# Decode attention and MLP in one launch: wq's load split 1 + 7 with x behind its first row, zero matmuls ahead of two stages, scores by quarters of K, one load counted on the rounds' semaphore

## The chip, the cores and the metric

The kernel runs on one core of one Trainium2 chip. A core has a matrix engine (TensorE, in the profile PE, its weight loads PEld), a vector engine (DVE), a scalar engine (ACT), GpSimd (POOL) and a synchronising engine (SP). All loads go through DMA queues that run on 16 DMA engines; a queue is fed by the engine that issues the transfer (in the profile SPq or ACTq). The metric is device time in microseconds (us) of one execution, as the median of several runs. A profiled execution gives a span, from the first to the last instruction, and that execution's own device time, which is a little longer than its span.

## The reference

One token is decoded, in bf16. `x` has 1024 elements and is layer-normed to `xn`. The result is `x + A(xn) + B(xn)`.

```
A:  q = xn @ wq                      # wq [1024, 4096], 32 heads of 128
    k, v = last 4096 rows of the caches, 4 kv heads, each shared by 8 heads
    p = softmax(q k^T / sqrt(128))
    return (p v) @ wo                # wo [4096, 1024]
B:  y = layernorm(xn)
    h = gelu(y @ w1 + b1)            # w1 [1024, 3584]
    return h @ w2 + b2               # w2 [3584, 1024]
```

Every weight is used once, so the work is 39.86 MB read from HBM for matrix products with one row: wq 8.39 MB, K 4.19, w1 7.34, V 4.19, w2 7.34, wo 8.39.

## The kernel before

All loops run over weights that are loaded once, in big transfers that SP issues in an order written out by hand (`load_chunks`, `load_k`, lines 155 to 161 and 230 to 237, and lines 308 to 319). One transfer takes several rows of the weight for each of the 128 partitions. The order is wq rows 0 to 3, K half 0, wq rows 4 to 7, K half 1, w1, both halves of V, w2 in two parts (16 and 12 chunks of 256 KB), wo in four parts (16, 11, 4 and 1 chunks of 256 KB). The three small rows x, b2 and b1 go out on ACT's queue at the very start (lines 165 to 170). A load signals a semaphore of its own by 16 when it has landed. Some issues wait: V overwrites K in SBUF, so both its halves wait for the last transposition of K (line 309); w2 overwrites wq, so it waits until q is done (line 312); wo waits until the product with w1 is done (line 314). SP takes its instructions in order, so a wait there holds back every later issue.

A product with one row is made with the weights as the moving operand, 512 columns at a time, and a nearly empty 128x128 stationary operand (XZ, YZ, GO) in which the one column in use is moved by the slice, so that each matmul adds its result into one row of a PSUM bank. `add` (line 429) records these matmuls, so most of PE's rows in the profile have line 430; they are told apart by tile: BIG,XZ is q (64 matmuls), KT,QBD the scores (32), BIG,YZ the product with w1, called h (56), KV,KT the product with V (32), BIG,GO the rounds and the tail.

PE's order is: x spread over partitions (line 426, waits for x's landing), q (lines 433 to 441), b1 and b2 and the mask put into PSUM (lines 443 to 457), scores (lines 460 to 469), h (lines 474 to 478), then the product with V, then eleven rounds (lines 497 to 503) of 8 matmuls each, seven over w2 and four over wo's first part, and then wo's last 16 chunks by matmuls of 32 columns, four at a time in the array (lines 512 to 528). PE waits on one counter, s_feed, in four places: for each half of wq, for each half of K, for each round. POOL adds to it: it waits for a load's own semaphore and then raises s_feed (lines 407 to 420).

DVE makes the layer norm of x (lines 257 to 275; XZ is done at the mark "xz"), transposes K in four quarters (`turn_k`, lines 282 to 287 and 306; three ahead of q's use and the last after it), copies q into the block diagonal QBD together with ACT (lines 298 to 305), and takes the maximum of the scores in two halves (line 330 to 333), from which the exponential follows on ACT and the transposition of p on DVE. POOL builds constants, to line 220, and QBD, XZ, GO are zeroed on it.

Of the kernel before, what the change touches and what calls it, by code (L numbers as in the profile page):

```python
# [9 lines left out]
D = 1024  # L10
# [7 lines left out]
FC = F // 128  # L18
KC = D // 128
NQ = HQ * DH  # L20
W1_CHUNKS = [8]
WQ_CHUNKS = [4, 4]
W2_CHUNKS = [16, 12]
WO_CHUNKS = [16, 11, 4, 1]
WO_HEAD = 1
XW = 136
PAIRS = 2
# [5 lines left out]
LEAD = 32  # L33
COPY = 64
ROUND = 4
ROUNDS = 11
STEP = 128

# [13 lines left out]
def bass_parallel_sum__sliding_block_cached__mixer_channel_mlp__decode_kernel(  # L52
# [17 lines left out]
    pe, dve, act, pool, sp = nc.tensor, nc.vector, nc.scalar, nc.gpsimd, nc.sync  # L70

    def sems(name, n):
        return [nc.alloc_semaphore(f"{name}{i}") for i in range(n)]

    s_x, s_b1, s_b2, s_v, s_out = (nc.alloc_semaphore(n) for n in ("s_x", "s_b1", "s_b2", "s_v", "s_out"))
    s_w1 = sems("s_w1", len(W1_CHUNKS))
    s_wq = sems("s_wq", len(WQ_CHUNKS))
    s_k = sems("s_k", PAIRS)
    s_wo = sems("s_wo", len(WO_CHUNKS))
    s_w2 = sems("s_w2", len(W2_CHUNKS))  # L80

    DVE = Track(nc, "S_DVE")
    ACT = Track(nc, "S_ACT")
    POOL = Track(nc, "S_POOL")
    done = {n: nc.alloc_semaphore(f"S_PE_{n}") for n in (
        "x", "h", "hT", "q", "sc", "pv", "tot", "fin")}
    s_feed = nc.alloc_semaphore("S_FEED")
# [5 lines left out]
    identb = sb("identb", [128, 128], bf16)  # L93
# [7 lines left out]
    OTHER = sb("OTHER", [2, 128], bf16)  # L101
    ALT = sb("ALT", [2, 512], bf16)
    EDGE = sb("EDGE", [2, 132], bf16)
    XBRP = sb("XBRP", [2, 16 * XP], bf16)
    B1R = sb("B1R", [32, F // 32], bf16)
# [6 lines left out]
    XZ = sb("XZ", [128, KC * XW], bf16)  # L112
    YZ = sb("YZ", [128, 192], bf16)
    QBD = sb("QBD", [128, PAIRS * 512], bf16)
# [15 lines left out]
    O2 = sb("O2", [128, 32], f32)  # L130
    GO = sb("GO", [128, ROUNDS * STEP + LEAD + 96], bf16)
    OT = GO[:, ROUNDS * STEP + LEAD:]
# [4 lines left out]
    BIG = sb("BIG", [128, KC * NQ + KC * F], bf16)  # L137
    WA, W1 = BIG[:, 0:KC * NQ], BIG[:, KC * NQ:KC * NQ + KC * F]
    W2 = WA[:, 0:FC * D]
    PS = nc.alloc_psum_tensor("PS", [128, 8 * 512], f32)  # L140
    PSb = PS[:, :].bitcast(bf16)

    def bank(n, rows=128, first=0):
        return PS[first:first + rows, n * 512:(n + 1) * 512]

    w1_p = B_w1.rearrange("(p r) n -> p r n", r=KC)
    wq_p = A_wq.rearrange("(p r) n -> p r n", r=KC)
    w2_p = B_w2.rearrange("(p c) n -> p c n", c=FC)
    wo_flat = A_wo.rearrange("(p j) n -> p (j n)", j=32)
# [3 lines left out]
    C = {}  # L153

    def load_chunks(dst, src, chunks, width, semaphores, c0=0):
        for j, n in enumerate(chunks):
            sp.dma_start(  # L157
                dst[:, c0 * width:(c0 + n) * width].rearrange("p (c n) -> p c n", c=n),
                src[:, c0:c0 + n, :],
            ).then_inc(semaphores[j], 16)  # L160
            c0 += n

    XB = XBRP[:, :].rearrange("p (a n) -> p a n", a=16)[:, :, 0:D // 16]

    def row_load(dst, src, semaphore):
        act.dma_start(dst, src.rearrange("o (a n) -> o a n", a=16)).then_inc(semaphore, 16)

    row_load(XB[0:1], A_x.rearrange("b s n -> (b s) n"), s_x)
    row_load(XB[1:2], B_b2.rearrange("(o n) -> o n", o=1), s_b2)
    act.dma_start(B1R[:, :], B_b1.rearrange("(p c) -> p c", p=32)).then_inc(s_b1, 16)  # L170

    def pool_wait():
        pool.wait_ge(POOL.sem, POOL.cnt)
# [45 lines left out]
    POOL.mark(pool.tensor_tensor(out=HALF[:, :], in0=HALF4[:, 0:2], in1=HALF4[:, 2:4], op=ALU.add))  # L219
    C["consts"] = POOL.cnt  # L220

    act.wait_ge(POOL.sem, C["QBD"])
    ACT.mark(act.activation(out=PS[:, 0:1024], in_=QBD[:, :], func=ACTF.Copy))
    ACT.mark(act.activation(out=bank(7), in_=QBD[:, 0:512], func=ACTF.Copy))
# [2 lines left out]
    def pairs(cache, c):  # L227
        return cache[0, 2 * c:2 * c + 2, SK - W:SK, :].rearrange("g (m i) d -> m g (i d)", m=64)

    def load_k(c):  # L230
        sp.dma_start(KV[:, c * 8192:(c + 1) * 8192], pairs(A_k_cache, c)).then_inc(s_k[c], 16)  # L231

    load_chunks(WA, wq_p, WQ_CHUNKS[:1], NQ, s_wq)
    load_k(0)
    load_chunks(WA, wq_p, WQ_CHUNKS[1:], NQ, s_wq[1:], WQ_CHUNKS[0])
    load_k(1)
    load_chunks(W1, w1_p, W1_CHUNKS, F, s_w1)

# [43 lines left out]
    def turn_k(n):  # L282
        dve.wait_ge(s_k[n // 2], 16)
        C["kt", n] = DVE.mark(dve.transpose(KT[:, n * 4096:(n + 1) * 4096], KV[:, n * 4096:(n + 1) * 4096]))  # L284

    for n in range(3):
        turn_k(n)

    act.wait_ge(done["q"], 8)
# [8 lines left out]
    for b in range(4):  # L298
        for c in range(PAIRS):
            to = QD[32 * b:32 * b + 32, c, :, b, 16 * c:16 * c + 16].rearrange("p e (u j) -> p e u j", j=4)  # L300
# [2 lines left out]
                C["d_QBD"] = DVE.mark(dve.tensor_copy(to, of))  # L303
            else:
                C["a_QBD"] = ACT.mark(act.activation(out=to, in_=of, func=ACTF.Copy))  # L305
    turn_k(3)

    V = KV[:, :]
    sp.wait_ge(DVE.sem, C["kt", 3])
    for c in range(PAIRS):  # L310
        sp.dma_start(V[:, c * 8192:(c + 1) * 8192], pairs(A_v_cache, c)).then_inc(s_v, 16)
    sp.wait_ge(done["q"], 8)
    load_chunks(W2, w2_p, W2_CHUNKS, D, s_w2)
    sp.wait_ge(done["h"], 7)
    c0 = 0
    for j, n in enumerate(WO_CHUNKS):
        first = (FC + c0) * D
        sp.dma_start(BIG[:, first:first + n * D], wo_flat[:, c0 * D:(c0 + n) * D]).then_inc(s_wo[j], 16)  # L318
        c0 += n

    def spread(first, n):
# [6 lines left out]

    S = PS[:, 3 * 512:7 * 512]
    for n in range(2):  # L330
        dve.wait_ge(done["sc"], 14 + 2 * n)
        C["mx"] = DVE.mark(dve.tensor_reduce(  # L332
            out=MX2[:, n:n + 1], in_=S[:, 1024 * n:1024 * n + 1024], axis=AX.X, op=ALU.max))
    dve_wait()
# [62 lines left out]
    for engine, track, a in ((act, ACT, 1), (dve, DVE, 0)):  # L397
        engine.wait_ge(done["fin"], 1)
        of, to = PS[64 * a:64 * a + 64, 7 * 512 + 256 * a:7 * 512 + 256 * a + 256], Pb[0:64, 256 * a:256 * a + 256]
# [4 lines left out]


    pool_wait()
    pool.wait_ge(s_wq[0], 16)
    pool.sem_inc(s_feed, 1)
    pool.wait_ge(s_wq[1], 16)
    pool.sem_inc(s_feed, 1)  # L410
    pool.wait_ge(DVE.sem, C["kt", 1])
    pool.sem_inc(s_feed, 1)
    pool.wait_ge(DVE.sem, C["kt", 3])
    pool.sem_inc(s_feed, 1)
    for semaphores, chunks in ((s_w2, W2_CHUNKS), (s_wo, WO_CHUNKS[:WO_HEAD])):
        if semaphores is s_wo:
            pool.wait_ge(ACT.sem, C["OT"])
        for semaphore, n in zip(semaphores, chunks):
            pool.wait_ge(semaphore, 16)
            pool.sem_inc(s_feed, n // ROUND)  # L420
    pe.wait_ge(POOL.sem, C["ones"])
    turn = pe.alloc_register("turn")
    pe.reg_mov(turn, 1)
    pe.wait_ge(s_x, 16)
    for i in range(2):
        last = pe.matmul(bank(2 + i), lhsT=onesb[0:1, :], rhs=XB[0:1, 8 * i:8 * i + 8, :])  # L426
    last.then_inc(done["x"], 1)

    def add(to, lhsT, rhs, **place):
        return pe.matmul(to, lhsT=lhsT, rhs=rhs, start=False, stop=False, skip_group_check=True, **place)  # L430

    pe.wait_ge(DVE.sem, C["xz"])
    with pe.Fori(0, len(WQ_CHUNKS)) as j:
        pe.wait_ge(s_feed, turn)
        pe.reg_add(turn, turn, 1)
        with pe.Fori(0, 4) as t:
            for u in range(2):
                for k in range(4):
                    last = add(bank(7), XZ[:, bass.ds(t * 2 + j * (4 * XW) + (XW * k + u), 128)],
                               WA[:, bass.ds(t * -1024 + j * (4 * NQ) + (k * NQ + (7 - u) * 512), 512)])  # L440
            last.then_inc(done["q"], 1)

    pe.wait_ge(s_b1, 16)
    turned = PS[:, 2 * 512 + 32:2 * 512 + 64].rearrange("p (c t) -> p c t", c=4)[:, :, 0:7]
    for q in range(4):
        pe.matmul(turned, lhsT=E4[:, q * 128:(q + 1) * 128],
                  rhs=B1R[:, q * FC:(q + 1) * FC].rearrange("p (t c) -> p c t", c=4),
                  start=(q == 0), stop=False, skip_group_check=True)
# [4 lines left out]
    for a in range(2):  # L453
        pe.matmul(bank(7), lhsT=EDGE[:, 1 - a:129 - a], rhs=XB[:, 8 * a:8 * a + 8, :], start=(a == 0), stop=False,
                  skip_group_check=True)
    for n in range(4):
        pe.matmul(bank(3 + n), lhsT=OTHER[:, :], rhs=ALT[:, :], start=True, stop=False, skip_group_check=True)
    pe.wait_ge(DVE.sem, C["d_QBD"])
    K4 = KT[:, :].rearrange("p (x k) -> p x k", k=128)
    with pe.Fori(0, PAIRS) as c:  # L460
        pe.wait_ge(s_feed, turn)
        pe.reg_add(turn, turn, 1)
        pe.wait_ge(ACT.sem, C["a_QBD"])
        with pe.Fori(0, 2) as j:
            for n in range(4):
                for u in range(2):
                    last = add(bank(3 + n), QBD[:, bass.ds(c * 512 + j * 256 + u * 128, 128)],
                               K4[:, bass.ds(c * 64 + 16 * n, 16), bass.ds(j * 64 + 32 * u, 32)])
                last.then_inc(done["sc"], 1)

    def h_cols(row, t):
        return row.rearrange("p (m a c) -> p m a c", m=128, a=7)[:, :, bass.ds(t, 1), :]
# [2 lines left out]
    with pe.Fori(0, 7) as t:  # L475
        for k in range(KC):
            last = add(bank(0), YZ[:, bass.ds(t + 8 * k, 128)], h_cols(W1[:, k * F:(k + 1) * F], t))
# [5 lines left out]
    for c in range(4):  # L483
        last = add(turned[:, c], H8[:, c:512:4], FLIP[:, 0:7])
# [6 lines left out]
    with pe.Fori(0, 8) as i:  # L491
        for u in range(4):
            last = add(bank(1), PT[:, bass.ds(i * 256 + u * 64, 128)], V3[:, :, bass.ds(i * 1024 + u * 256, 256)])
# [2 lines left out]
    pe.wait_ge(DVE.sem, C["d_GT"])  # L496
    with pe.Fori(0, ROUNDS) as t:
        pe.wait_ge(s_feed, turn)
        pe.reg_add(turn, turn, 1)
        for u in range(ROUND):  # L500
            for a in range(2):
                add(bank(7), GO[:, bass.ds(t * STEP + (LEAD + 2 * u - ROW - a), 128)],
                    BIG[:, bass.ds(t * (ROUND * D) + (u * D + a * 512), 512)])

    c0 = TAIL
# [54 lines left out]
```

## Time and profile before

| | |
|---|---|
| median of 3 runs | 99.41 us (99.19 to 99.42) |
| profiled execution | 99.37 us, span 97.4 us |
| PE busy | 73.0 us of the span (354 matmuls) |
| DVE busy | 38.9 us |
| ACT, POOL busy | 11.2 us, 9.9 us |
| bytes | 39.86 MB read, 409 GB/s over the span |
| SP's DMA queue | its packets' time is 95.7% of 16 engines' span |

The page gives, for each engine, the busy time in the span, then the span in 40 equal slices (each 2.4 us) with the busy share in tenths, the granted clock of PE in tenths, the busy share of the DMA engines and the GB/s they moved. Then it follows the chain of work that ended last back from the last instruction. Groups of instructions are listed by line and tile with their mean duration and what ended the idle time before them. DMA issues are listed with the time from the start of the issue to the landing. Matmuls overlap, so the duration of one (380 ns) is longer than the distance between two (about 216 ns at the full clock).

### The profile page before, as it was taken

What the parts mean: (1) busy time and instruction counts of PE and PEld (TensorE: products, weight loads), DVE (VectorE), ACT (ScalarE), POOL (GpSimd) and SP (SyncE); (2) the same over time, 40 slices, a digit from 0 to 9 for tenths busy, and PEclk for the clock granted to TensorE, in tenths of its full rate; (3) what the DMA queues carried; (4) which work ended last, traced back from release to release, by engine and by line L of the source; (5) the groups of instructions that cost most, each with busy time, mean ns of one, the idle gap of its engine ahead of it and who ended that gap; (6) DMA issues with size and microseconds to landing.
All of it is one profiled execution on the core that took longest, in us unless ns stands there. A gap on an engine that the chain in (4) does not pass through costs nothing.

```text
span 97.4 us, 1285 instructions
## 1 busy us (share of the span) xinstructions
PE 73.0 (75%) x354; PEld 30.4 (31%) x354; DVE 38.9 (40%) x54; ACT 11.2 (12%) x20; POOL 9.9 (10%) x27
## 2 busy tenths in 40 slices
PE   0004000099999986999979999799999999779992
PEld 0000000033444431333434444333343443334450
DVE  0002899899930799940293620050048000000001
ACT  0880000600000024000005200200000000000001
POOL 6999400000000000000000000000000000000000
PEclk9999999999999998557999999999999999999999
DMA  7599999999999998888999999999999999899890
GB/s 215 256 431 431 405 432 444 431 444 431 410 431 481 636 424 377 377 377 377 437 431 431 437 498 431 431 444 394 394 464 498 431 431 431 376 435 426 372 377 1
DMA packets 1989, 39.88 MB, mean 409 GB/s; under 512 B 322, under 2 KB 324, under 8 KB 452
## 3 DMA queue, kind: packets, MB, share of 16 engines
q1 hardware_dynamic: 1876, 39.85, 95.7%
q10 hardware_dynamic: 112, 0.01, 0.1%
q8 instruction: 1, 0.02, 0.1%
HBM read 39.86 MB, written 0.00 MB: 409 GB/s over the span
## 4 chain that ended last, share of the span: by engine, by line
DMA 80%; PE 14%; SPq 3%; issue 1%; DVE 0%
DMA BIG<-in_B_w_dram 47%; DMA BIG<-in_A_wo_dram 33%; PE PS L430 13%; SPq L231 1%; SPq L157 1%; SPq L318 1%; DVE Pb L400 0%; PE PS L507 0%
## 5 line engine op out<-in xcount | busy, mean ns | idle before, releaser
L430 PE MATMUL PS<-BIG,XZ 128*128 x64 | 16.5, 427 | 10.2 <-DVE B L277 10.2
L430 PE MATMUL PS<-BIG,GO 128*128 (+1 forms) x148 | 22.2, 337 | 1.4 <-POOLq L420 1.2
L284 DVE STREAM_TRANSPOSE KT<-KV 128x4096 bf16<-128x4096 bf16 x4 | 17.6, 4432 | 4.8 <-DMA KV<-in_A_k_cache_dram 4.8
L430 PEld LDWEIGHTS PS<-BIG,GO 128*128 (+1 forms) x148 | 9.9, 97 | 13.8 <-issue 6.4
L430 PEld LDWEIGHTS PS<-BIG,XZ 128*128 x64 | 6.9, 108 | 20.3 <-issue 14.3
L430 PE MATMUL PS<-BIG,YZ 128*128 x56 | 12.4, 380 | 0.6 <-DMA BIG<-in_B_w_dram 0.6
L430 PE MATMUL PS<-KT,QBD 128*128 x32 | 10.0, 491 | 1.0 <-ACT QBD L305 1.0
L430 PE MATMUL PS<-KV,KT 128*128 x32 | 8.3, 381 | 0.5
L400 DVE CAST Pb<-PS 64x256 bf16<-64x256 f32 x1 | 0.4, 417 | 20.4 <-PE PS L507 20.4
L430 PEld LDWEIGHTS PS<-BIG,YZ 128*128 x56 | 5.4, 96 | 7.6 <-issue 1.8
L426 PE MATMUL PS<-XBRP,onesb 1*128 1x512 bf16 x2 | 1.0, 616 | 8.1 <-DMA XBRP<-in_A_x_dram 8.1
L430 PEld LDWEIGHTS PS<-KT,QBD 128*128 x32 | 3.8, 120 | 7.2 <-issue 5.2
L244 DVE BATCH_NORM_STATS2 BN<-PS 128x6 f32<-128x512 f32 x2 | 1.3, 689 | 9.1 <-PE PS L426 9.1
L430 PEld LDWEIGHTS PS<-KV,KT 128*128 x32 | 3.1, 96 | 5.3 <-issue 3.8
L332 DVE TENSOR_REDUCE MX<-PS 128x1 f32<-128x1024 f32 x2 | 2.4, 1220 | 5.6 <-PE PS L430 5.6
L379 DVE SCALAR_TENSOR_TENSOR QBD<-PS,REC,HALF 32x256 f32<-32x256 f32 x2 | 0.9, 474 | 6.9 <-PE PS L430 6.8
L344 ACT ACTIVATE Pb<-PS,NMB 128x2048 bf16<-128x2048 f32 x1 | 2.0, 1968 | 13.8 <-DVE NMB L341 13.8
L348 DVE STREAM_TRANSPOSE KT<-Pb 128x2048 bf16<-128x2048 bf16 x1 | 2.3, 2311 | 2.1 <-ACT Pb L344 2.1
L353 DVE COPY HT<-PS 128x28 f32<-128x28 f32 x1 | 0.2, 210 | 6.4 <-PE PS L430 6.4
L400 ACT ACTIVATE Pb<-PS 64x256 bf16<-64x256 f32 x1 | 0.4, 381 | 20.1 <-PE PS L507 20.1
L426 PEld LDWEIGHTS PS<-XBRP,onesb 1*128 1x128 bf16 x2 | 0.1, 104 | 8.1 <-DMA XBRP<-in_A_x_dram 8.1
L290 ACT ACTIVATE Pb<-PS 128x512 bf16<-128x512 f32 x1 | 0.6, 597 | 16.6 <-PE PS L430 16.6
(77 smaller groups left out, 37.7 us busy)
## 6 DMA issues: line engine op xcount, KB each, us to landing
BIG<-in_A_wq_dram SPq DMA_DIRECT2D x2, 4096.0 KB, 18.8
BIG<-in_B_w_dram SPq DMA_DIRECT2D x1, 7168.0 KB, 46.0
KV<-in_A_k_cache_dram SPq DMA_DIRECT2D x2, 2048.0 KB, 23.1
KV<-in_A_v_cache_dram SPq DMA_DIRECT2D x2, 2048.0 KB, 13.6
BIG<-in_B_w_dram SPq DMA_DIRECT2D x1, 4096.0 KB, 24.8
BIG<-in_A_wo_dram SPq DMA_DIRECT2D x1, 4096.0 KB, 23.5
BIG<-in_B_w_dram SPq DMA_DIRECT2D x1, 3072.0 KB, 31.4
BIG<-in_A_wo_dram SPq DMA_DIRECT2D x1, 2816.0 KB, 29.8
```

The source lines that it names most:

```text
L157: sp.dma_start(dst[:, c0 * width:(c0 + n) * width].rearrange("p (c n) -> p c n", c=n), src[:, c0:c0 + n, :],).then_inc(semaphores[j], 16)
L231: sp.dma_start(KV[:, c * 8192:(c + 1) * 8192], pairs(A_k_cache, c)).then_inc(s_k[c], 16)
L244: DVE.mark(dve.bn_stats(out=BN[:, 12 * n + 6 * i:12 * n + 6 * i + 6], in_=src[:, 512 * i:512 * i + 512]))
L284: C["kt", n] = DVE.mark(dve.transpose(KT[:, n * 4096:(n + 1) * 4096], KV[:, n * 4096:(n + 1) * 4096]))
L318: sp.dma_start(BIG[:, first:first + n * D], wo_flat[:, c0 * D:(c0 + n) * D]).then_inc(s_wo[j], 16)
L332: C["mx"] = DVE.mark(dve.tensor_reduce(out=MX2[:, n:n + 1], in_=S[:, 1024 * n:1024 * n + 1024], axis=AX.X, op=ALU.max))
L344: C["exp"] = ACT.mark(act.activation(out=Pb[:, :], in_=S, func=ACTF.Exp, bias=NMB[:, 0:1], scale=SCALE, accum_out=SUMP[:, 0:1]))
L348: C["d_pt"] = DVE.mark(dve.transpose(PT[:, 0:2048], Pb[:, :]))
L379: DVE.mark(dve.scalar_tensor_tensor(out=ONM.rearrange("p (i c d) -> p i c d", i=2, c=PAIRS)[:, i], in0=PS[rows, 512:1024].rearrange("p (c ...
L400: track.mark(act.activation(out=to, in_=of, func=ACTF.Copy) if a else dve.tensor_copy(to, of))
L426: last = pe.matmul(bank(2 + i), lhsT=onesb[0:1, :], rhs=XB[0:1, 8 * i:8 * i + 8, :])
L430: return pe.matmul(to, lhsT=lhsT, rhs=rhs, start=False, stop=False, skip_group_check=True, **place)
```

## The change

- wq is loaded as one row for each partition (1 MB) and then seven (7 MB), both on one semaphore, both ahead of K. The load of x moves from ACT's queue to SP's, between the two. The loads of b2 and b1 stay on ACT's queue and wait for POOL's `identb`.
- q waits for both parts of wq directly (no s_feed) and runs in eight groups of 8 matmuls, each group over all eight rows of wq for 512 columns.
- A function `busy` adds matmuls whose stationary and moving operands are zero. 38 of them (19 times 2) run ahead of q, after POOL's constants; 8 run among the four mask matmuls ahead of the scores.
- Two quarters of K are transposed ahead of q's use, two after. The scores run by quarters of K: each waits for its own transposition, and the two halves of the maximum wait for 3 and 4 quarters in place of 14 and 16 groups.
- V's first half waits for K's second quarter, its second half for the fourth.
- s_feed counts 32 for each round. wo's first load adds its 16 to it directly, POOL the other 16 when the attention's output is ready, and then the remaining three rounds.
- wo is loaded as 16, 10, 5 and 1 chunks in place of 16, 11, 4 and 1.

```diff
-WQ_CHUNKS = [4, 4]
+WQ_CHUNKS = [1, 7]
-WO_CHUNKS = [16, 11, 4, 1]
+WO_CHUNKS = [16, 10, 5, 1]
+HALF_FEED = 16
...
-    s_wq = sems("s_wq", len(WQ_CHUNKS))
+    s_wq = [nc.alloc_semaphore("s_wq")] * len(WQ_CHUNKS)
...
-    row_load(XB[0:1], A_x.rearrange("b s n -> (b s) n"), s_x)
-    row_load(XB[1:2], B_b2.rearrange("(o n) -> o n", o=1), s_b2)
-    act.dma_start(B1R[:, :], B_b1.rearrange("(p c) -> p c", p=32)).then_inc(s_b1, 16)
...
+    act.wait_ge(POOL.sem, C["identb"])
+    row_load(act, XB[1:2], B_b2.rearrange("(o n) -> o n", o=1), s_b2)
+    act.dma_start(B1R[:, :], B_b1.rearrange("(p c) -> p c", p=32)).then_inc(s_b1, 16)
...
     load_chunks(WA, wq_p, WQ_CHUNKS[:1], NQ, s_wq)
+    row_load(sp, XB[0:1], A_x.rearrange("b s n -> (b s) n"), s_x)
+    load_chunks(WA, wq_p, WQ_CHUNKS[1:], NQ, s_wq, WQ_CHUNKS[0])
     load_k(0)
-    load_chunks(WA, wq_p, WQ_CHUNKS[1:], NQ, s_wq[1:], WQ_CHUNKS[0])
     load_k(1)
...
-    for n in range(3):
+    for n in range(2):
         turn_k(n)
...
-    turn_k(3)
+    for n in range(2, 4):
+        turn_k(n)
...
-    sp.wait_ge(DVE.sem, C["kt", 3])
     for c in range(PAIRS):
+        sp.wait_ge(DVE.sem, C["kt", 2 * c + 1])
         sp.dma_start(V[:, c * 8192:(c + 1) * 8192], pairs(A_v_cache, c)).then_inc(s_v, 16)
...
-        sp.dma_start(BIG[:, first:first + n * D], wo_flat[:, c0 * D:(c0 + n) * D]).then_inc(s_wo[j], 16)
+        sp.dma_start(BIG[:, first:first + n * D], wo_flat[:, c0 * D:(c0 + n) * D]).then_inc(s_wo[j] if j else s_feed, HALF_FEED)
...
-        dve.wait_ge(done["sc"], 14 + 2 * n)
+        dve.wait_ge(done["sc"], 3 + n)
...
+    for semaphore, n in zip(s_w2, W2_CHUNKS):
+        pool.wait_ge(semaphore, 16)
+        pool.sem_inc(s_feed, 2 * HALF_FEED * (n // ROUND))
+    pool.wait_ge(ACT.sem, C["OT"])
+    pool.sem_inc(s_feed, HALF_FEED)
+    pool.wait_ge(s_feed, 2 * HALF_FEED * (FC // ROUND + 1))
+    pool.sem_inc(s_feed, 2 * HALF_FEED * (WO_CHUNKS[0] // ROUND - 1))
...
+    def busy(zeros, to, **how):
+        for i in range(2):
+            pe.matmul(to, lhsT=zeros[:, 0:128], rhs=zeros[:, 0:512], skip_group_check=True, **how)
+
+    pe.wait_ge(POOL.sem, C["consts"])
+    with pe.Fori(0, 19):
+        busy(QBD, bank(4), start=True, stop=True)
     pe.wait_ge(DVE.sem, C["xz"])
...
+    with pe.Fori(0, 8) as t:
+        pe.wait_ge(s_wq[0], 16 * len(WQ_CHUNKS))
+        for k in range(KC):
+            last = add(bank(7), XZ[:, bass.ds(t + XW * k, 128)], WA[:, bass.ds(t * -512 + (k * NQ + 7 * 512), 512)])
+        last.then_inc(done["q"], 1)
...
+    with pe.Fori(0, 4) as n:
+        pe.matmul(PS[:, bass.ds(n * 512 + 3 * 512, 512)], lhsT=OTHER[:, :], rhs=ALT[:, :], start=True, stop=False,
+                  skip_group_check=True)
+        busy(GO, bank(1), start=False, stop=False)
...
+        with pe.Fori(0, 2) as i:
+            pe.wait_ge(DVE.sem, turn)
+            pe.reg_add(turn, turn, 1)
+            for n in range(2):
+                for j in range(2):
+                    for u in range(2):
+                        last = add(PS[:, bass.ds(i * 1024 + (3 + n) * 512, 512)],
+                                   QBD[:, bass.ds(c * 512 + (j * 256 + u * 128), 128)],
+                                   K4[:, bass.ds(c * 64 + i * 32 + 16 * n, 16), j * 64 + 32 * u:j * 64 + 32 * u + 32])
+            last.then_inc(done["sc"], 1)
...
         pe.wait_ge(s_feed, turn)
-        pe.reg_add(turn, turn, 1)
+        pe.reg_add(turn, turn, 2 * HALF_FEED)
```

More of the change, by code (lines that the diff above doesn't have):

```diff
@@ L163, in bass_parallel_sum__sliding_block_cached__mixer_channel_mlp__decode_kernel, with row_load @@
     XB = XBRP[:, :].rearrange("p (a n) -> p a n", a=16)[:, :, 0:D // 16]
-    def row_load(dst, src, semaphore):
-        act.dma_start(dst, src.rearrange("o (a n) -> o a n", a=16)).then_inc(semaphore, 16)
-    row_load(XB[0:1], A_x.rearrange("b s n -> (b s) n"), s_x)
-    row_load(XB[1:2], B_b2.rearrange("(o n) -> o n", o=1), s_b2)
-    act.dma_start(B1R[:, :], B_b1.rearrange("(p c) -> p c", p=32)).then_inc(s_b1, 16)
+    def row_load(engine, dst, src, semaphore):
+        engine.dma_start(dst, src.rearrange("o (a n) -> o a n", a=16)).then_inc(semaphore, 16)
     def pool_wait():
@@ L406, in bass_parallel_sum__sliding_block_cached__mixer_channel_mlp__decode_kernel @@
     pool_wait()
[L407 to L421, printed above, removed]
+    for semaphore, n in zip(s_w2, W2_CHUNKS):
[5 more added lines that the diff above has]
+    pool.sem_inc(s_feed, 2 * HALF_FEED * (WO_CHUNKS[0] // ROUND - 1))
+    pe.wait_ge(POOL.sem, C["QBD"])
     turn = pe.alloc_register("turn")
-    pe.reg_mov(turn, 1)
+    pe.reg_mov(turn, C["kt", 0])
     pe.wait_ge(s_x, 16)
@@ L430, in add @@
         return pe.matmul(to, lhsT=lhsT, rhs=rhs, start=False, stop=False, skip_group_check=True, **place)
-    pe.wait_ge(DVE.sem, C["xz"])
-    with pe.Fori(0, len(WQ_CHUNKS)) as j:
-        pe.wait_ge(s_feed, turn)
-        pe.reg_add(turn, turn, 1)
[L436 to L441, printed above, removed]
+    def busy(zeros, to, **how):
[4 more added lines that the diff above has]
+        busy(QBD, bank(4), start=True, stop=True)
+    pe.wait_ge(DVE.sem, C["xz"])
+    with pe.Fori(0, 8) as t:
[3 more added lines that the diff above has]
+        last.then_inc(done["q"], 1)
     pe.wait_ge(s_b1, 16)
@@ L455, in bass_parallel_sum__sliding_block_cached__mixer_channel_mlp__decode_kernel @@
                   skip_group_check=True)
-    for n in range(4):
-        pe.matmul(bank(3 + n), lhsT=OTHER[:, :], rhs=ALT[:, :], start=True, stop=False, skip_group_check=True)
+    with pe.Fori(0, 4) as n:
+        pe.matmul(PS[:, bass.ds(n * 512 + 3 * 512, 512)], lhsT=OTHER[:, :], rhs=ALT[:, :], start=True, stop=False,
+                  skip_group_check=True)
+        busy(GO, bank(1), start=False, stop=False)
     pe.wait_ge(DVE.sem, C["d_QBD"])
@@ L460, in bass_parallel_sum__sliding_block_cached__mixer_channel_mlp__decode_kernel @@
     with pe.Fori(0, PAIRS) as c:
-        pe.wait_ge(s_feed, turn)
-        pe.reg_add(turn, turn, 1)
         pe.wait_ge(ACT.sem, C["a_QBD"])
[L464 to L469, printed above, removed]
+        with pe.Fori(0, 2) as i:
[8 more added lines that the diff above has]
+            last.then_inc(done["sc"], 1)
+        pe.reg_add(turn, turn, C["kt", 2] - C["kt", 1] - 1)
+    pe.reg_mov(turn, 2 * HALF_FEED)
     def h_cols(row, t):
@@ L498, in bass_parallel_sum__sliding_block_cached__mixer_channel_mlp__decode_kernel @@
         pe.wait_ge(s_feed, turn)
-        pe.reg_add(turn, turn, 1)
+        pe.reg_add(turn, turn, 2 * HALF_FEED)
         for u in range(ROUND):
```

## The prediction

> **What bounds the kernel now.** I read the page's slices first, then the chain that ended last, then each load's landing, then the engines' timeline for the slack. Page of the profile (span and slices) and its account of queues:
>
> ```profile
> span 97.4 us, 1285 instructions
> PEclk9999999999999998557999999999999999999999
> GB/s 215 256 431 431 405 432 444 431 444 431 410 431 481 636 424 377 377 377 377 437 431 431 437 498 431 431 444 394 394 464 498 431 431 431 376 435 426 372 377 1
> q1 hardware_dynamic: 1876, 39.85, 95.7%
> ```
>
> SP's queue is busy 95.7% of 97.4 us, 93.2 us; about 2 us are missing at each end and nothing between. The loads' issues (size, time from the start of the issue to the landing) and the end of the chain, in order of time:
>
> ```profile
> BIG<-in_B_w_dram SPq DMA_DIRECT2D x1, 7168.0 KB, 46.0
> BIG<-in_A_wo_dram SPq DMA_DIRECT2D x1, 4096.0 KB, 23.5
> BIG<-in_A_wo_dram SPq DMA_DIRECT2D x1, 2816.0 KB, 29.8
> BIG<-in_A_wo_dram SPq DMA_DIRECT2D x1, 1024.0 KB, 31.8
> BIG<-in_A_wo_dram SPq DMA_DIRECT2D x1, 256.0 KB, 32.0
> ```
>
> ```profile
> 62.92 31.79 DMA BIG<-in_A_wo_dram
> 94.72 0.04 issue
> 94.76 0.62 PE PS L430 x16
> 95.38 0.02 issue
> 95.40 0.30 PE PS L507 x4
> 95.70 0.02 issue
> 95.72 0.42 DVE Pb L400
> ```
>
> wo's parts were issued at 62.08, 62.45, 62.92 and about 63.4, so they landed at 85.6, 92.3, 94.7 and 95.4. The first half of wq (issue 0.81, asked for alone 12.1 us) landed at 12.9. From there to 95.4 the other 35.66 MB took 82.5 us, 432 GB/s throughout. The kernel is one unbroken stream of loads, about 2 us before it and 2.0 us of tail behind 95.4. So an edit counts if it moves the stream's start, opens a gap in it, or makes PE too late for the last landings. PE's slack in the timeline:
>
> ```profile
> 19.33 16.55 PE L430 MATMUL PS<-BIG,XZ 128*128 x64 [10.22 <-DVE B L277]
> 24.42 9.23 PEld L430 LDWEIGHTS PS<-BIG,XZ 128*128 x43 [0.28 <-issue]
> 38.14 4.45 DVE L284 STREAM_TRANSPOSE KT<-KV 128x4096 bf16<-128x4096 bf16 x1
> 49.61 12.44 PE L430 MATMUL PS<-BIG,YZ 128*128 x56 [0.57 <-DMA BIG<-in_B_w_dram]
> 85.92 9.46 PE L430 MATMUL PS<-BIG,GO 128*128 x92 [1.18 <-POOLq L420]
> 93.23 1.10 PEld L430 LDWEIGHTS PS<-BIG,GO 128*32 128x32 bf16 x44 [0.42 <-issue]
> 94.76 0.34 PEld L430 LDWEIGHTS PS<-BIG,GO 128*32 128x32 bf16 x16 [0.43 <-DMA BIG<-in_A_wo_dram]
> 95.10 0.11 PEld L517 LDWEIGHTS <-GO 128*32 128x32 bf16 x4
> ```
>
> From h at 49.61 on PE works without a real pause until it waits 1.18 us for wo's first part and 0.43 us for the third. Those two are what a later h can use up.
>
> **The change part by part.**
>
> *Start of the stream.* SP still issues wq at 0.81. x's issue (0.58 us on ACT before) now stands between wq's two; wq's second issue ends near 2.6 instead of 1.9, and w1's near 4.5 instead of 3.9. The first megabyte keeps the queue busy until about 5, so this costs 0; uncovered it would be 0.58. Bytes are equal. One row of wq is an 8 KB run for each partition, 64 KB apart; wo's third part has the same runs at the same distance, and its megabyte took 92.3 to 94.7, 2.4 us or 430 GB/s. What the trace can't show is another first transfer. In 1 to 3 us the stream moved 360 and 164 KB, 0.52 MB where 0.86 go at 432 GB/s: 0.8 us short, of which 0.2 lie ahead of the end of wq's issue at 1.2. Ends: -0.6 if smaller runs avoid the rest, +0.6 if the start were paid again behind x. I take 0, because the nearest row, 6 to 12 us with the small packets of x, b2 and b1 in it, moved 526, 524, 526, 360, 263 and 429 GB/s, a mean of 438: small packets cost the stream nothing.
>
> *x, layer norm, ACT.* x landed at 8.0, on a queue of its own. Now it follows the first megabyte: 12.9 less 3 MB at 2.43 us is 5.6. The chain from x to XZ took 10.4 us (8.08 to 18.46), so XZ is ready near 16. ACT issues b2 and b1 (0.6 + 0.7 us) only after identb, at 2.56, so its first table load moves from 2.80 to 3.9 and its square-root table is ready near 8.1 instead of 6.94, when the variance is due (5.6 + 1.05 + 1.29 + 0.5 = 8.4): 0. b1 and b2 are wanted near 37. All of it is hidden, because q now waits for something later.
>
> *q.* All of wq, 8.39 MB, lands at 12.9 + 4.19/0.432 = 22.6, against a start of q at 19.33. POOL's constants end at 11.0, so the 38 zero matmuls start there. Before, q's matmuls stood 0.427 us apart until 24.4, and 0.215 from then (9.23/43): the gate opened 5.1 us after q began. With 12 zero matmuls at 0.427 and 26 at 0.216 they take 10.7 us, to 21.7 (8 to 16 slow ones: 20.9 to 22.6), ahead of wq. q then runs at full clock: h's 56 matmuls are 12.44 us, so 64 take 14.2. From 22.9 (0.25 from landing to first matmul, as with h) it ends at 37.1, against 35.9: +1.2 us.
>
> *K, scores.* K's first half lands with wq's old second half at 27.5, so quarters one and two are done by 27.5 + 8.76 = 36.3, before q. After q, QBD's copying took 2.2 us (35.91 to 38.14); quarters three and four then run 39.3 to 48.1, where the last one ended at 42.6. Eight zero matmuls (1.7 us) and the mask run from 37.7 to about 41; QBD is ready near 40, so scores start 1 us late, but their first three quarters (24 matmuls, 5.2 to 6.7 us) end by 47.7 and the last one has to wait for 48.1 anyway: 0. If that transposition were early, they would cost 1.
>
> The last quarter: 0.4 us of register work (38.15 to 38.98 before holds two such), 8 matmuls at 0.216 to 0.28 (the latter if the sequencer can't run ahead), 0.4 to 0.6 to leave the loops and begin h. So h begins at 50.6 to 51.2, not 49.61: 1.0 to 1.6 us late. The maximum's first half now runs ahead of that, so the exponential and p's transposition end near 58, before V's product at 64: 0.
>
> *Does that reach the end?* No: 1.18 + 0.43 us of waits, plus 0.10 for 40 narrow matmuls where 44 were (1.10/44 each), plus 0.1 at the last part: 20 loads take 0.43 where 16 took 0.34, then 0.11, so 95.3 against the landing at 95.4. Slack 1.8 against 1.0 to 1.6. The fifth chunk in wo's third part costs 0 by the same sum.
>
> *Queue waits on SP.* V's first half is issued at 36.3 (before 42.6), its second at 48.1, w2 from 48.7, wo near 63.4. w1 lands at 49.3 and a half of V lasts 4.9 us, so the second half is needed by 53, w2 by 58, wo by 75: no gap, with 5 us to spare. POOL's wait took 85.62 to 85.69, so counting directly saves under 0.1, inside the slack.
>
> Sum: 99.37 for the profiled execution (97.4 plus 1.97 around it), 0.04 below the median, plus 0: 99.4.
>
> **The rivals.** A difference below 0.3%, 0.3 us, can hardly be told from none here.
>
> 1. *PE too late* (the other side). If h starts over 1.8 us late, each further tenth is on the path: the last quarter of the scores is the place. The first weight loads of the scores stood 0.28 us apart near 39; if the output bank, which now moves too, adds 0.1 to each of 8 (an estimate: one more register step) and 0.3 are lost between the zero matmuls and q, lateness is 2.1 to 2.7 and the time 99.7 to 100.3. For it: the margin is only 0.2 to 0.8. Against it: h and q keep 0.22 for each matmul in loops of 8.
>
> 2. *The clock gate.* Either the zero matmuls don't open it, and q pays 12 x 0.21 = 2.5 us again (h 3.8 late, 2.0 over, 101.4), or it falls in a gap ahead of the last quarter (0.3 to 1.9 us) and 8 to 16 matmuls of scores and h pay 0.21 each: 1.7 to 3.4, over by 1.2 to 3.2. For it: the granted clock was 0.50 from 38.2 to 45.0 although PE was never idle over 0.96 us; between 35.9 and 38.2 it ran only matmuls of 1 to 32 rows. Against: from 83.0 to 86.4 PE was busy 2.22 of 3.40 us and the clock stayed 1.00. The Trainium skill, "TensorE: Matmul & The Clock Gate" (Part 1), lets the gate fall only after an idle window of some 3.4 us; by that rule the second case never happens and this rival keeps only its first. The trace contradicts a rule of idle time alone, so I don't lower it.
>
> 3. *A better start*: the 0.6 us above falls away, wholly or by half: 98.8 to 99.1. For it: 0.52 MB in 2 us. Against: nothing says the run's length causes that.
>
> 4. *The strided row is slow.* At half the rate the first megabyte costs 2.4 us more, on the stream: 101.8. [...] wo's third part speaks against it.
>
> **How the numbers follow.** No change that reaches the end 0.60 (its own range 99.1 to 99.7); PE late 0.12; gate 0.13; start 0.13; slow row 0.02. Faster 0.13, same 0.60, slower 0.12 + 0.13 + 0.02 = 0.27. The range takes in the better start and PE late, and the milder half of the gate's: 98.8 to 101.0.
>
> **What would show it.** Right: x at 5.6, wq at 22.6, q 22.9 to 37.1 with matmuls 0.216 apart, the last transposition to 48.1, h from about 51, the wait ahead of wo's first part almost gone, wo's last landings at 94.7 and 95.4 as before. Wrong: any of those landings moved (start), a granted clock of 0.50 in q or after 46 us, or no wait left ahead of wo's third part.

## The result, and the profile after

The changed kernel takes 100.21 us (median; 99.6 to 100.68) against 99.12 us (98.75 to 99.42) for the kernel before: a ratio of 1.0106, 95% interval 1.0076 to 1.0136. It is slower, by about 1 us, where no change was forecast. The profiled execution took 100.22 us, its span is 98.8 us.

The page after, span, slices and SP's queue:

```profile
span 98.8 us, 1412 instructions
PEclk9999999999999999859999999999999999999999
GB/s 70 634 326 465 396 373 395 371 405 418 444 424 557 541 371 395 371 418 557 265 424 431 431 484 424 424 424 405 448 448 411 424 424 438 439 406 410 406 240 2
q1 hardware_dynamic: 1908, 39.85, 94.8%
```

The queue moved the same 39.85 MB, but was busy for 94.8% of 98.8 us in place of 95.7% of 97.4. The next two fences are the end of the chain in order of time, and the loads (size, time from the start of the issue to the landing):

```profile
63.73 0.33 SPq L320
64.06 0.04 issue
64.10 0.43 SPq L320
64.54 0.04 issue
64.58 31.55 DMA BIG<-in_A_wo_dram
96.13 0.04 issue
96.17 0.73 PE PS L425 x20
96.91 0.20 PE PS L511 x4
97.10 0.02 issue
97.13 0.42 DVE Pb L402
```

```profile
BIG<-in_A_wq_dram SPq DMA_DIRECT2D x1, 1024.0 KB, 4.7
BIG<-in_A_wq_dram SPq DMA_DIRECT2D x1, 7168.0 KB, 21.8
BIG<-in_A_wo_dram SPq DMA_DIRECT2D x1, 4096.0 KB, 23.1
BIG<-in_A_wo_dram SPq DMA_DIRECT2D x1, 256.0 KB, 31.7
```

The kernel still ends on wo's landings, and these are later: the third part at 64.58 + 31.55 = 96.1, where it was 94.7, the last at 96.8, where it was 95.4. That is +1.4 us, the whole of the span's 1.4. 1.1 us of it is already there at wq: the second load, issued at 1.94, landed at 1.94 + 21.8 = 23.7, where 22.6 was forecast. The rest came later, 0.17 us of it for each DMA engine in packets near 87 us, of which the last section tells.

PE, DVE and the issue of wq in the timeline after:

```profile
1.28 0.62 SPq L167 DMA_DIRECT2D XBRP<-in_A_x_dram  x1
1.94 0.57 SPq L158 DMA_DIRECT2D BIG<-in_A_wq_dram  x1
17.23 5.06 PEld L429 LDWEIGHTS PS<-QBD 128*128 128x128 bf16 x24 [0.28 <-issue]
23.86 13.98 PE L425 MATMUL PS<-BIG,XZ 128*128 x64 [1.08 <-DMA BIG<-in_A_wq_dram]
39.97 8.77 DVE L285 STREAM_TRANSPOSE KT<-KV 128x4096 bf16<-128x4096 bf16 x2
51.27 12.44 PE L425 MATMUL PS<-BIG,YZ 128*128 x56
87.05 8.55 PE L425 MATMUL PS<-BIG,GO 128*128 x68 [0.74 <-POOLq L415]
96.17 0.45 PEld L425 LDWEIGHTS PS<-BIG,GO 128*32 128x32 bf16 x20 [0.86 <-DMA BIG<-in_A_wo_dram]
```

h begins at 51.27, 1.66 us later than before, and yet PE waits 0.74 us for wo's first part and again for the third. PE isn't what is late.

The trace also records each landing by DMA engine (16 for each load) and each packet; a packet of wq's second load is one partition's run of it, 56 KB. wq's second load landed on 15 engines between 22.3 and 23.0 and on the sixteenth at 23.70. wo's last part landed on 15 between 95.4 and 96.0 and on the sixteenth at 96.76. One engine had fallen 0.7 us behind the others before 24 us, and at each later load, for 73 us, one landed 0.6 to 0.8 us behind the fifteenth; the landings do not say which, but so steady a distance points to the same one. The packet records say when: the first packets of wq's second load, from 4.55 on, directly behind x, took 0.39 us longer on the mean of the engines than the usual 2.12, on the worst 1.15 longer. Before, no load but the very first had such packets.

### The profile page after: what moved, and what is told of

It is laid out like the page before. It is cut to its first block, busy times and chain, and to the rows that moved or that the text cites. A ratio compares the mean times of both kernels' runs of the same rounds, so it can differ in the third digit from the quotient of the medians.

```text
span 98.8 us, 1412 instructions
## 1 busy us (share of the span) xinstructions
PE 81.8 (83%) x389; PEld 34.0 (34%) x400; DVE 39.1 (40%) x54; ACT 11.2 (11%) x20; POOL 10.5 (11%) x27
## 3 DMA queue, kind: packets, MB, share of 16 engines
q1 hardware_dynamic: 1908, 39.85, 94.8%
## 4 chain that ended last, share of the span: by engine, by line
DMA 54%; PE 40%; SPq 2%; issue 1%; ACT 1%; DVE 0%
PE PS L425 35%; DMA BIG<-in_A_wo_dram 32%; DMA BIG<-in_A_wq_dram 22%; PE PS L429 3%; PE PS L455 1%; SPq L320 1%; SPq L167 1%; ACT Pb L291 1%; PE PS L452 1%; DVE Pb L402 0%; SPq L158 0%; PE PS L511 0%
## 5 line engine op out<-in xcount | busy, mean ns | idle before, releaser
L425 PE MATMUL PS<-BIG,GO 128*128 (+1 forms) x137 | 21.5, 334 | 2.0 <-POOLq L415 0.7
L429 PE MATMUL PS<-QBD 128*128 128x512 bf16 x38 | 11.1, 463 | 5.0 <-POOL HALF L216 5.0
L425 PE MATMUL PS<-BIG,XZ 128*128 x64 | 14.0, 379 | 1.1 <-DMA BIG<-in_A_wq_dram 1.1
L425 PEld LDWEIGHTS PS<-BIG,XZ 128*128 x64 | 6.2, 98 | 8.8 <-issue 2.5
L429 PEld LDWEIGHTS PS<-QBD 128*128 128x128 bf16 x38 | 4.2, 113 | 12.2 <-issue 9.5
L425 PE MATMUL PS<-KT,QBD 128*128 x32 | 7.9, 402 | 0.0
L425 PEld LDWEIGHTS PS<-KT,QBD 128*128 x32 | 3.3, 104 | 4.8 <-issue 1.9
L429 PE MATMUL PS<-GO 128*128 128x512 bf16 x8 | 3.2, 493 | 0.0
## 6 DMA issues: line engine op xcount, KB each, us to landing
BIG<-in_A_wq_dram SPq DMA_DIRECT2D x1, 7168.0 KB, 21.8
```

The source lines that it names most:

```text
L429: pe.matmul(to, lhsT=zeros[:, 0:128], rhs=zeros[:, 0:512], skip_group_check=True, **how)
```

## The experiments

Each ratio is to the kernel before, timed beside the run (its medians there were 98.88 to 98.95 us). A landing is that of the slowest engine in the profiled execution.

**Theories.** S: the stream's start is paid twice, in the first packets behind x, and a load signals only when its slowest engine is done. P: PE is too late through the last quarter of the scores (the first rival of the prediction). S splits by its cause: x's place (S1), the step from runs of 8 KB for each partition to runs of 56 KB (S2), or b2's and b1's small packets (S3).

**The old start of loads under the new kernel.** [4, 4] rows, x, b2 and b1 on ACT's queue at once; all else as changed.

```diff
-WQ_CHUNKS = [1, 7]
+WQ_CHUNKS = [4, 4]
+    row_load(act, XB[0:1], A_x.rearrange("b s n -> (b s) n"), s_x)
+    row_load(act, XB[1:2], B_b2.rearrange("(o n) -> o n", o=1), s_b2)
+    act.dma_start(B1R[:, :], B_b1.rearrange("(p c) -> p c", p=32)).then_inc(s_b1, 16)
...
-    act.wait_ge(POOL.sem, C["identb"])
-    row_load(act, XB[1:2], B_b2.rearrange("(o n) -> o n", o=1), s_b2)
-    act.dma_start(B1R[:, :], B_b1.rearrange("(p c) -> p c", p=32)).then_inc(s_b1, 16)
...
-    row_load(sp, XB[0:1], A_x.rearrange("b s n -> (b s) n"), s_x)
```

> The changed kernel with the start of loads of before: wq as 4 + 4 rows, x, b2 and b1 on ACT's queue at once; all else as changed. Theory S (the stream's start is paid twice and one DMA engine stays about 0.7 us behind): the last landing goes back from 96.8 to about 95.4 and the time to that of before, ratio 0.998 to 1.003. Rival P (PE too late through the last quarter of the scores): the time stays near 1.010.

Measured: 0.9998 (0.9984 to 1.0012), last landing 95.7. P falls: q behind all of wq (landed at 22.6), the late transpositions, the zero matmuls and the new split of wo together cost nothing. The whole loss lies in the start of the loads.

**Only x back on ACT's queue.**

```diff
+    row_load(act, XB[0:1], A_x.rearrange("b s n -> (b s) n"), s_x)
...
-    row_load(sp, XB[0:1], A_x.rearrange("b s n -> (b s) n"), s_x)
```

> Only x goes back to ACT's queue at the start; wq stays 1 + 7, b2 and b1 stay behind identb. If x between the two loads of wq makes the bubble (S1): ratio near 1.000 or below, down to 0.997, because the first packets of 8 KB cost 0.3 us less than those of 32 KB. If the step from 8 KB runs to 56 KB runs makes it (S2): ratio stays 1.006 to 1.011. P: 1.010.

Measured: 1.0002 (0.9988 to 1.0015). SP's issues and the loads:

```profile
0.81 0.87 SPq L158 DMA_DIRECT2D BIG<-in_A_wq_dram  x2
BIG<-in_A_wq_dram SPq DMA_DIRECT2D x1, 7168.0 KB, 21.4
XBRP<-in_A_x_dram ACTq DMA_DIRECT2D x1, 2.0 KB, 4.7
```

Both loads of wq are issued by 1.68, the second lands by 22.7, and x lands at 5.5, as early as on SP's queue. S2 falls: 8 KB runs with 56 KB runs behind them are still there. x on SP's queue is the cause, but not yet in which way.

**Only the split back to 4 + 4.** x stays on SP between the halves.

```diff
-WQ_CHUNKS = [1, 7]
+WQ_CHUNKS = [4, 4]
```

> Only wq's split goes back to 4 + 4; x stays on SP between the two, so it lands near 13 instead of 5.6 and XZ near 24, so that q starts near 24 instead of 23.9. S1: the packets behind x are late again, only later, ratio 1.004 to 1.010. S2: the stream is as before and PE at most 0.3 us later, ratio 1.000 to 1.004. P: 1.010 to 1.015.

Measured: 1.0068 (1.0039 to 1.0097). By its ratio alone this would be S1, and that would be wrong. In its profile wq landed by 22.6, the last part of wo at 95.6, and no packet behind x was slow. What is late there is PE: x lands at 13.2, and the zero matmuls stand behind x's on PE. PE in its timeline:

```profile
24.41 13.98 PE L425 MATMUL PS<-BIG,XZ 128*128 x64
49.80 1.90 PE L425 MATMUL PS<-KT,QBD 128*128 x8 [1.46 <-DVE KT L285]
83.80 12.05 PE L425 MATMUL PS<-BIG,GO 128*128 x105
```

q begins at 24.4, h at 51.8 (2.2 us later than before), and from there on PE waits for no load. So P is real with h this late; it is not what the change suffers from, where PE still waits. The profiled execution is this kernel's shortest (99.10 of 99.10 to 100.05 us), so how late PE was in the longer ones, and whether PE alone made them longer, isn't shown.

**b2 and b1 early.**

```diff
+    row_load(act, XB[1:2], B_b2.rearrange("(o n) -> o n", o=1), s_b2)
+    act.dma_start(B1R[:, :], B_b1.rearrange("(p c) -> p c", p=32)).then_inc(s_b1, 16)
...
-    act.wait_ge(POOL.sem, C["identb"])
-    row_load(act, XB[1:2], B_b2.rearrange("(o n) -> o n", o=1), s_b2)
-    act.dma_start(B1R[:, :], B_b1.rearrange("(p c) -> p c", p=32)).then_inc(s_b1, 16)
```

> Only b2 and b1 go back to the start of ACT's queue (without the wait for identb); x and wq as changed. If the late engine comes from b2's and b1's small packets between packets of 56 KB (S3): the spread of the landings of wq's second load shrinks from 1.4 us to about 0.5 and the ratio to 1.002 to 1.005. S1 and S2: nothing changes, 1.010.

Measured: 1.0100 (1.0075 to 1.0125), one engine 0.6 us behind the others at wq and 0.8 at the end. S3 falls. The run also shows what one engine does: on the mean of the engines wo's last part landed at 95.37, as with the old start of loads (95.37 too), on the slowest at 96.39 against 95.73.

**Two ways in which x could do it.** D: x's issue delays the issue of wq's second load, which then comes too shortly before the queue gets to it. X: x's small packets break the stream. A larger first load tells them apart, and a late issue without x.

```diff
-WQ_CHUNKS = [1, 7]
+WQ_CHUNKS = [2, 6]
```

> The changed kernel with wq as 2 + 6 rows, x still between them on SP's queue. If the bubble behind x comes from wq's second load being issued too late for a queue that is nearly dry (theory D), 2 MB of cover leave its descriptors waiting 2.4 us longer: no excess in its first packets, the last landing near 95.5, ratio 0.999 to 1.003. If x's small packets themselves break the stream wherever they stand in it (theory X): the bubble moves to 7.5 us and stays, ratio 1.006 to 1.010.

```diff
+    row_load(act, XB[0:1], A_x.rearrange("b s n -> (b s) n"), s_x)
...
-    row_load(sp, XB[0:1], A_x.rearrange("b s n -> (b s) n"), s_x)
+    sp.wait_ge(POOL.sem, C["QBD"])
     load_chunks(WA, wq_p, WQ_CHUNKS[1:], NQ, s_wq, WQ_CHUNKS[0])
```

> x on ACT's queue at the start, wq as 1 + 7, and SP waits for POOL's zeroed QBD before it issues the second load, so that this goes out near 2.05, as late as in the changed kernel (1.94), without x ahead of it. Theory D: the bubble is back without x, ratio 1.005 to 1.011. Theory X: none, ratio 0.999 to 1.002.

Measured: 1.0004 (0.9987 to 1.0021) with 2 + 6 and x in between, 1.0125 (1.0110 to 1.0141) with the late issue and x elsewhere. Both go D's way. SP's issues in the latter (the first line holds both loads of wq and the wait between them) and its loads:

```profile
0.81 1.58 SPq L158 DMA_DIRECT2D BIG<-in_A_wq_dram  x2
BIG<-in_A_wq_dram SPq DMA_DIRECT2D x1, 1024.0 KB, 4.8
BIG<-in_A_wq_dram SPq DMA_DIRECT2D x1, 7168.0 KB, 21.5
XBRP<-in_A_x_dram ACTq DMA_DIRECT2D x1, 2.0 KB, 5.0
```

**The lead varied with 2 + 6.** SP waits for a later or an earlier mark of POOL before the second load of wq; x stays in between.

```diff
-WQ_CHUNKS = [1, 7]
+WQ_CHUNKS = [2, 6]
...
-    POOL.mark(pool.memset(ALT[:, :], 0.0))
+    C["hold"] = POOL.mark(pool.memset(ALT[:, :], 0.0))
...
+    sp.wait_ge(POOL.sem, C["hold"])
     load_chunks(WA, wq_p, WQ_CHUNKS[1:], NQ, s_wq, WQ_CHUNKS[0])
```

> wq as 2 + 6 rows with x between them, and SP waits for POOL's zeroed ALT (4.7 us) before it issues the second load, which ends near 5.2. The first 2 MB keep the queue until about 7. Theory D (a load has to be issued some 2.5 us before the queue gets to it): 1.8 us of lead are too few, the stream loses 0.5 to 1.2 us there, ratio 1.005 to 1.013. If only a first transfer of 1 MB, or its 8 KB runs, makes the loss: ratio 1.000, as with 2 + 6 alone.

The second takes the mark of FLIP's zeroing instead of ALT's.

> The same with the wait on an earlier mark of POOL (3.9 us), so that the second load's issue ends near 4.5 and leads by 2.5 us. Theory D: little or no loss, ratio 0.999 to 1.004, and between the runs with 2.0 and with 4.5 us of lead. If any late issue costs alike: 1.005 or more.

Measured: 1.0124 (1.0093 to 1.0155) and 1.0001 (0.9981 to 1.0021). The issue of wq's second load, first in the late, then in the middle run:

```profile
4.71 0.34 SPq L158 DMA_DIRECT2D BIG<-in_A_wq_dram  x1
```

```profile
3.93 0.34 SPq L158 DMA_DIRECT2D BIG<-in_A_wq_dram  x1
```

0.78 us decide over 1.2%. The runs side by side; lead is from the end of the issue of wq's second load to its first packet, the excess is what the first packet of each engine took over its usual time, both from the packet records, the landings are those of the slowest engine:

| kernel | lead us | excess us, mean and worst engine | wq landed | wo's last landed | ratio |
|---|---|---|---|---|---|
| changed | 2.04 | 0.39, 1.15 | 23.70 | 96.76 | 1.0106 |
| b2 and b1 early | 2.25 | 0.14, 0.77 | 23.28 | 96.39 | 1.0100 |
| late issue, x on ACT | 2.22 | 0.76, 1.19 | 23.57 | 96.27 | 1.0125 |
| 2 + 6, late | 2.24 | 0.47, 1.16 | 23.99 | 96.69 | 1.0124 |
| x on ACT | 2.88 | 0.01, 0.10 | 22.68 | 95.49 | 1.0002 |
| 2 + 6, middle | 3.00 | 0.00, 0.00 | 22.59 | 95.61 | 1.0001 |
| 2 + 6 | 4.78 | 0.00, 0.00 | 22.69 | 95.58 | 1.0004 |

In this table a lead of 2.0 to 2.25 us costs 0.8 to 1.2 us on the worst engine, one of 2.9 or more 0.1 us at most, whatever the first load's size, its runs, or x's place.

The ratios 1.0125 and 1.0124 are not the loads' alone. In the profiles of the late issue and of the late 2 + 6 PE ran to the end with no wait, or one of 0.2 us. In the late 2 + 6 PE had stood idle for 2.78 us ahead of q, and its granted clock was 0.50 from 25.22 to 28.64:

```profile
24.15 15.67 PE L426 MATMUL PS<-BIG,XZ 128*128 x64 [2.78 <-DMA BIG<-in_A_wq_dram]
75.49 21.80 PE L426 MATMUL PS<-BIG,GO 128*128 x148
```

q took 1.7 us longer than the 13.98 of the middle run, h began at 53.25, and PE's rounds set the end. Three of its six executions show a mean granted clock of 1.000 and took 99.61 to 100.25 us, still 0.7 to 1.3 us more than the kernel before. The changed kernel and the one with b2 and b1 early end on wo's landings instead.

V's second half, which waits for the last transposition, shows the same further on. Its issue in the late 2 + 6, then in the run without zero matmuls (below):

```profile
50.75 0.54 SPq L314 DMA_DIRECT2D KV<-in_A_v_cache_dram  x1
```

```profile
49.74 0.54 SPq L314 DMA_DIRECT2D KV<-in_A_v_cache_dram  x1
```

The leads there were 2.78 and 2.82 us (first packets at 54.07 and 53.09), and the worst packets were 0.50 and 1.03 us long beyond their usual 0.61; with 3.45 us, in the run with 4 + 4, there was no excess. Whether one limit, just under 2.9 us, holds for both loads no run tests.

What happens in the engines in those 2 to 3 us no run shows. The Trainium skill, "DMA: Bandwidth & Descriptors" (Latency and other measured facts), gives about 0.6 us to the first byte of a load issued from SP and up to 2 us for an access to HBM at high load; their sum, 2.6 us, is an estimate that lies between the two groups of the table but below the 2.78 and 2.82 us that still cost, and no run here separates these parts.

**wo's split**, from the version with x on ACT's queue:

```diff
-WO_CHUNKS = [16, 10, 5, 1]
+WO_CHUNKS = [16, 11, 4, 1]
```

> x on ACT's queue at the start, wq as 1 + 7, and wo back to 16, 11, 4 and 1 chunks. In every run with 10 chunks the packets of 20 KB near 87 us took up to 0.2 us for each DMA engine too long, those of 22 KB before did not. If the size does it: the last landing is 0.1 to 0.2 us earlier, ratio 0.998 to 0.999. If not, ratio 1.000.

Measured: 0.9999 (0.9981 to 1.0018). The packets near 87 us are at their usual time again and the last landing of the profile is 95.19 instead of 95.49, but the time shows no gain within its interval. The expected gain was missed, or is too small to be seen.

**No zero matmuls ahead of q**, from the same version:

```diff
-    with pe.Fori(0, 19):
-        busy(QBD, bank(4), start=True, stop=True)
```

> x on ACT's queue at the start, wq as 1 + 7, without the 38 zero matmuls ahead of q (they compute nothing that is used). If they are what opens the gate: q's first 8 to 16 matmuls stand 0.427 us apart again, h begins 1.7 to 3.4 us later than 50.2, 0.5 to 2.5 us over PE's slack, ratio 1.005 to 1.025. If the gate is no concern, ratio 1.000.

Measured: 1.0093 (1.0065 to 1.0122). q in this run, then in the one with x on ACT's queue and the zero matmuls:

```profile
22.72 16.08 PE L426 MATMUL PS<-BIG,XZ 128*128 x64 [16.14 <-DMA BIG<-in_A_wq_dram]
```

```profile
22.84 13.98 PE L426 MATMUL PS<-BIG,XZ 128*128 x64 [0.84 <-DMA BIG<-in_A_wq_dram]
```

Without them q is 2.1 us longer, h begins at 52.2 and PE is late. A second effect came with it: V's second half, issued by 50.27 behind the late transposition, led by 2.82 us only, and wo's last part landed at 96.44 instead of 95.49. PE's rounds with the narrow matmuls behind them, and the load at which the chain ends:

```profile
74.52 22.06 PE L426 MATMUL PS<-BIG,GO 128*128 x148
```

```profile
65.54 30.26 DMA BIG<-in_A_wo_dram
```

Where PE never waited, in the late 2 + 6, the same matmuls took 21.80 us, so some 0.3 us of the 1.0 us by which the span grew (98.5 against 97.5) were waits for late loads and the rest PE's, an estimate from two profiled executions. So the zero matmuls earn about what they were forecast to earn, given that q starts so late, but not all of this ratio is theirs.

No version beat the kernel before: the best of them are at its time. What is left in all of them is the unbroken stream.

## Why the prediction was wrong

*The step that failed* is the first, the start of the stream: "The first megabyte keeps the queue busy until about 5, so this costs 0; uncovered it would be 0.58". The issue ended at 2.51, as forecast (2.6), and the queue did reach it at 4.55. But the cover was reckoned as if an issued load were ready at once. With 2.04 us between, the first packets were 0.39 us late on the mean and 1.15 on the worst engine. The upper end of the bounds, "+0.6 if the start were paid again behind x", names the event; the value taken was 0, and the end was too small: it was reckoned from the bytes of all engines together, a mean, where the slowest engine decides. The row that was taken as nearest, 6 to 12 us of the kernel before, held small packets of another queue ahead of loads that had been issued long before; it could say that small packets are harmless, which is right, and nothing of a short lead.

*The range* held the median by luck: its upper part stood there for PE and the clock gate, which cost nothing here, while this cause had only the +0.6, in no rival and with no chance. The sign that came, wq's and wo's landings moved, is one that the prediction had named.

*x, layer norm*: x landed at 5.6 as forecast. *Zero matmuls*: 11.06 us against 10.7, the gate open from about 17 (24 loads in 5.06, 0.21 apart). *q*: 13.98 us against 14.2, and its start was late by wq's landing, 23.86 against 22.9. (From that landing to the first matmul it was 0.16 us, not 0.25; with h, from which the 0.25 was taken, the chain of before has 0.35.) *K, scores*: the last transposition ended at 48.7 against 48.1, h began at 51.27 against 50.6 to 51.2. The slack of 1.8 us can't be read from the changed kernel: h was 1.66 us late and PE still waited for both of wo's parts, but these landed 1.4 us late themselves. With 4 + 4 and x on SP they landed nearly in time, and h 2.2 us late left no wait; that fits a slack near 1.8.

*The clock gate*: the granted clock fell once more, in spite of the zero matmuls among the mask. Two windows of the changed kernel (us, PE, PEld, DVE, ACT, POOL busy with counts, granted clock, DMA share, GB/s):

```profile
38.00:41.00 3.00, 2.53 (x13) 0.62 (x10) 2.39 (x6) 1.49 (x5) 0.00 (x0) 1.00 1.37 593
41.00:44.00 3.00, 3.00 (x8) 0.78 (x8) 3.00 (x1) 0.00 (x0) 0.00 (x0) 0.52 0.75 325
```

It fell behind 3 us in which PE was busy 2.53. The Trainium skill, "TensorE: Matmul & The Clock Gate" (Part 1), has it fall after an idle window of about 3.4 us; this trace doesn't agree. It did no harm here: with 2 + 6 the profile shows the same fall (0.50 from 40.07 to 43.48) at a ratio of 1.0004, and three of the nine executions of the changed kernel had a mean granted clock of 1.000 and still took 100.08 to 100.42 us. In the late 2 + 6, where it fell inside q, it made q 1.7 us longer.

*A better start* came in part: the first packets' excess was 0.3 us for each engine instead of 0.6, yet with x on ACT's queue the time is 1.0002: the spread between engines took it back. There wq landed at 22.21 on the mean of the engines against 22.42 with the old start of loads, but on the slowest at 22.68 against 22.62. *The strided row*: no run shows it at half the rate; the first megabyte landed at 4.9 to 5.5, as forecast (5.6).

## What to carry to other kernels

In a kernel that is one stream of loads, an issue isn't hidden because the queue still has work when it comes: in these runs it had to end about 3 us before the queue got to it, so what is put ahead of it on the issuing engine counts as soon as the load in front is short. Look at the slowest of the 16 DMA engines, not at the mean: what one engine had lost by 24 us was still missing at the end, and each later load waited for it. Before a delay is blamed on what was moved, move the delay alone; here the small load was innocent and its 0.62 us of issue were not.

## What was not expected of the hardware

A load whose issue ended 2.0 to 2.25 us ahead of its first packet lost 0.8 to 1.2 us on its worst engine and 0.1 to 0.8 us on the mean, one with 2.9 us or more 0.2 us at most on any. In the changed kernel the loss of the slowest engine was kept from 24 us to the end (0.69 us behind the fifteenth at wq, 0.76 at wo's last part).

In the kernels that load 10 chunks of wo at once (20 KB for each partition), packets near 87 us ran 0.07 to 0.23 us long for each engine in total, in every profile but those of the late issue and the late 2 + 6; with 11 chunks (22 KB) they didn't. Its cause stays open, and its effect on the time is below what the runs resolve.
